# Two-piece split of keys, values and whole w_out blocks, and attention of the first unit ahead of later weight columns

## Chip, cores and metric

The kernel runs on one core of a Trainium2 chip. The metric is the device time of one launch in microseconds (us); lower is better. The engines are PE (TensorE, matmuls; PEld is its weight loads), DVE (VectorE), ACT (ScalarE), POOL (GpSimd) and SP (SyncE, which here only issues DMAs). Each engine works through its own list of instructions in a fixed order.

## The reference, cut to what is computed

```python
# attention: batch 4, heads 8, sequence 576, head size 64
scores = q @ k.T / 8
bias   = relu(x @ w1 + b1) @ w2      # x: a fixed function of the two positions; one bias per head
attn   = softmax(scores + bias)
x      = (attn @ v), heads side by side     # 2304 tokens x 512
# first feed-forward, hidden 1536
h = silu(x @ w_gate) * (x @ w_val);  x = h @ w_out
# second feed-forward, hidden 2048
h = relu(x @ w_in);  out = (h * h) @ w2_out
```

The large inputs of the feed-forwards are 64-bit numbers; keys, values and queries are 32-bit. Precision is kept by splitting each matrix into a 16-bit high part and a 16-bit low part ("hi" and "lo") and multiplying three of the four pairs.

## The kernel before, in words

**Units.** The 2304 tokens are worked in nine units of 256. A unit is one quarter of the sequence for two of the four batches (unit 8 holds the 64 last positions of all batches). `attend` makes the attention of a round: round 0 is the first sequence quarter for all four batches, and gives units 0 and 1. It has 32 steps, one per batch and head. In a step PE multiplies queries with keys (`scores`, L772), DVE adds the bias and finds the minimum (L780), ACT takes the exponential (L785) and its 16-bit part (L792), POOL the rest (L220, tile `pt`), an SP transpose turns both (L801, tile `pT`), and PE multiplies with the values (L812, two steps later). After 16 steps a unit is complete: `finish_unit` scales it and transposes it into `xT` (L857, L860).

**Keys and values.** For round 0 they come in eight groups of four heads (`h` 0 to 7). `load_kv` loads a group as 128 partitions x (4 heads x 4 rows x 64) and a tail of 64 partitions x (4 heads x 64). `prep_k` and `prep_v` split them with `halves`, in five chunks of 4 x 64 columns (`kv_chunks`). `halves` has three ways: way 1 makes hi on POOL (L197) and lo on DVE (L191); way 0 makes hi on ACT (L201) and lo on DVE (L191); way 2 scales on ACT (L205), makes hi on ACT (L209) and lo on POOL (L220). `MIX` says which: values always take way 1, key chunks take 0 and 2 in turn. Key chunks are then transposed by PE (`turn`, L686). Round 0 reads keys and values from these tiles (`wr`, `kva`, `kvb`); copies go to `kT_d` and `v_d` in HBM for the later rounds. `feed_first` calls the preparation of group h+1 at steps 4h (keys) and 4h+2 (values).

**Weights.** `w_stream` loads w_gate and w_val in three column blocks of 512 (`first`), then w_out in 12 row blocks of 128 x 512 (`second`, key "o"). Each block is decoded from 64-bit to 32-bit by three DVE operations (`decode`, L256, L259, L261), its columns' norms are taken, and it is split by `halves`. w_out blocks are decoded in two pieces of 256 columns, from four staging rooms in `wst`; from its eighth block on w_out waits for the last group's values ("kv", 8).

**moe1(m)** makes the first feed-forward of unit m: L453 for gate and val (needs `xT` of the unit and the weights' column block), L476 for w_out (needs all of w_out). `make_bias(t)` makes the bias of a round: masks on DVE (L597), matmuls on PE (L635), L611 and L617 on ACT, L612 and L618 on POOL. weights2 and the second feed-forward follow when all attention is done.

**What sets the order.** These parts are generators that yield a cost after each piece. `merge` takes the one whose sum of costs, divided by its weight, is least; `a_all` merges attention at weight 25.5 with the weights at 70. The lines of the loop at L1234 then mix that with moe1. The result is the program order; a list scheduler turns it into one list per engine with this order as the priority.

## Time and profile before

| | us |
|---|---|
| median of 3 runs | 1310.92 (1310.74 to 1312.64) |
| the profiled execution, its own time | 1316.36 |
| span of the profiled execution | 1314.6 |
| busy in that span: PE, DVE, ACT, POOL | 1105.3, 882.9, 633.6, 772.4 |

A profile row that groups instructions has the line, engine, operation and tiles, then the count, busy time in us, mean ns of one, and the engine's idle time just before with what ended it. The duration of an instruction on DVE or POOL includes time in which it has begun and cannot proceed. The view by stretches gives for each stretch of the span the busy time of every engine, the granted PE clock (1.00 is 2.4 GHz) and the mean busy share of the 16 DMA engines.

### The profile page before, as it was taken

Reading aid. Unit: us, or ns where it says so; the run is one execution under the profiler, and the core shown is the slowest. Engines: PE = TensorE matmul, PEld = TensorE weight load, DVE = VectorE, ACT = ScalarE, POOL = GpSimd, SP = SyncE. Lnnn points to the kernel's source line nnn. Section 1 sums busy time; section 2 is a strip of 40 time slices with the busy share of each in tenths; the row PEclk is TensorE's granted clock in tenths of the full one; section 3 lists DMA queues with packets and bytes.
Section 4 is the critical chain, followed back from the end, with each engine's and each line's share of the span. In section 5 each row is a group of like instructions: output and inputs, shape, how many; then the busy total and the mean of one; then the engine's idle time right before and its main releaser. Section 6 shows DMA issues by size and latency. Waiting matters only on the chain.

```text
span 1314.6 us, 27829 instructions
## 1 busy us (share of the span) xinstructions
PE 1105.3 (84%) x10676; PEld 806.6 (61%) x10676; DVE 882.9 (67%) x2042; ACT 633.6 (48%) x1316; POOL 772.4 (59%) x844
## 2 busy tenths in 40 slices
PE   3345556869899999999899987789977999999998
PEld 2334435656777868687685765647435658485687
DVE  6988887898666555657474533887788392754835
ACT  5546666647565565556565442437512341413322
POOL 4867644696986586757766450323898280724623
PEclk9998557769999999999999899899988999999999
DMA  8749997832999899998989994573001010020000
GB/s 235 184 125 186 227 239 187 189 84 52 214 216 215 184 198 178 196 212 171 183 176 202 228 232 118 180 213 96 16 0 33 33 33 33 0 49 17 17 34 16
DMA packets 329089, 177.47 MB, mean 135 GB/s; under 512 B 285052, under 2 KB 295292, under 8 KB 328956
## 3 DMA queue, kind: packets, MB, share of 16 engines
q1 hardware_dynamic: 328956, 175.70, 59.1%
q8 instruction: 83, 1.36, 0.4%
q14 instruction: 50, 0.41, 0.1%
HBM read 92.21 MB, written 19.48 MB: 85 GB/s over the span
## 4 chain that ended last, share of the span: by engine, by line
PE 44%; DVE 19%; DMA 16%; POOL 9%; issue 6%; ACT 4%; SPq 1%; POOLq 0%; ACTq 0%; DVEq 0%
PE mm L1290 11%; PE mm L1322 10%; PE mm L453 9%; PE mm L476 6%; DMA pT<-pt 5%; DMA qT<-qs 3%; PE av L812 3%; POOL pt L220 2%; PE qk L772 2%; DVE mask L597 2%; PE ma L1322 2%; DMA w2s<-in_moe_w_out_dram 1%; DVE wr L261 1%; DVE wr L191 1%; DVE s L780 1%
## 5 line engine op out<-in xcount | busy, mean ns | idle before, releaser
L453 PE MATMUL mm<-xT,wr 128*128 128x256 f16 x2376 | 297.2, 283 | 16.7 <-DVE th L464 10.3
L453 PEld LDWEIGHTS <-wr 128*128 128x128 f16 x2592 | 256.1, 101 | 69.6 <-issue 28.3
L1102 POOL TENSOR_TENSOR x<-x 128x256 f32<-128x256 f32 (+1 forms) x160 | 157.6, 993 | 155.2 <-ACT x L1299 149.9
L220 POOL TENSOR_TENSOR pt<-s,pt 128x576 f16<-128x576 f32 x144 | 189.3, 1317 | 69.0 <-ACT pt L792 58.0
L1290 PE MATMUL mm<-wr,w2r 128*128 128x512 f16 (+1 forms) x960 | 191.7, 362 | 10.6 <-ACT x L1295 10.6
L220 POOL TENSOR_TENSOR z<-th,z 128x256 f16<-128x256 f32 x108 | 83.9, 777 | 136.5 <-ACT z L438 133.6
L1290 PEld LDWEIGHTS <-w2r 128*128 128x128 f16 x960 | 94.7, 99 | 105.5 <-issue 16.2
L780 DVE CUSTOM_DVE_ANT_0 s<-qk,bias 128x576 f32<-128x576 f32 x144 | 107.7, 750 | 68.3 <-PE qk L772 47.1
L785 ACT ACTIVATE s<-s,sc 128x576 f32<-128x576 f32 x144 | 110.3, 772 | 88.8 <-DVE sc L784 74.3
L476 PE MATMUL mm<-wr,z 128*128 128x512 f16 x576 | 135.8, 380 | 1.9 <-DVE th L464 1.3
L812 PEld LDWEIGHTS <-pT 128*128 128x128 f16 (+3 forms) x2400 | 97.4, 104 | 57.4 <-DMA pT<-pt 34.0
L1322 PEld LDWEIGHTS <-wr 128*128 128x128 f16 x1134 | 111.0, 98 | 17.6 <-DVE wr L1102 2.5
L612 POOL TENSOR_TENSOR btmp<-btmp,xs 128x256 f32<-128x256 f32 (+1 forms) x108 | 81.7, 758 | 43.2 <-ACT btmp L611 39.4
L597 DVE TENSOR_TENSOR mask<-tabT,bias 128x1024 f16<-128x1024 f16 (+1 forms) x108 | 95.7, 901 | 12.3 <-PE ma L635 9.5
L812 PE MATMUL av<-vp,pT 128*128 128x65 f16 (+7 forms) x1920 | 85.4, 194 | 20.0 <-DMA pT<-pt 18.3
L1295 ACT ACTIVATE x<-mm 128x512 f32<-128x512 f32 (+1 forms) x80 | 43.4, 553 | 121.1 <-DVE wr L1102 69.4
L476 PEld LDWEIGHTS <-z 128*128 128x128 f16 x648 | 59.8, 98 | 65.1 <-issue 2.1
L1107 DVE CAST wr<-x 128x768 f16<-128x768 f32 (+3 forms) x60 | 61.1, 1022 | 36.0 <-ACT x L1299 22.9
L618 POOL TENSOR_TENSOR bias<-bias,btmp 128x256 f32<-128x256 f32 (+1 forms) x108 | 81.0, 752 | 5.9
L1102 DVE TENSOR_TENSOR wr<-x,wr 128x768 f16<-128x768 f32 (+3 forms) x60 | 80.4, 1343 | 1.9
L635 PEld LDWEIGHTS <-mask 128*128 128x128 f16 x1440 | 61.8, 106 | 30.5 <-issue 11.3
L1341 ACT ACTIVATE ob<-ob,fac 128x256 f32<-128x256 f32 x36 | 18.1, 507 | 108.0 <-DVE ob L1340 107.9
(257 smaller groups left out, 2038.5 us busy)
## 6 DMA issues: line engine op xcount, KB each, us to landing
vp<-v_d SPq DMA_DIRECT2D x64, 325.0 KB, 3.6
kp<-kT_d SPq DMA_DIRECT2D x64, 288.0 KB, 3.5
w2s<-in_moe_w_in_dram SPq DMA_DIRECT2D x16, 512.0 KB, 4.7
w2s<-in_moe_w_out_dram SPq DMA_DIRECT2D x16, 512.0 KB, 4.5
wr<-in_moe_w_gate_dram SPq DMA_DIRECT2D x24, 256.0 KB, 5.5
wst<-in_moe_w_out_dram SPq DMA_DIRECT2D x24, 256.0 KB, 4.0
wr<-in_moe_w_val_dram SPq DMA_DIRECT2D x24, 256.0 KB, 4.9
y_d<-yh SPq DMA_DIRECT2D x18, 256.0 KB, 3.8
```

What stands on the lines that cost most here:

```text
L220: nc.gpsimd.tensor_tensor(out=out_, in0=x, in1=hi, op=ALU.subtract)
L453: nc.tensor.matmul(pg[:, 256 * gi:256 * gi + 256], wr.parts(key, f // 4, cc, wl, P * (f % 4), P), mov(xl, cc), start=k == 0, stop=k == 11)
L476: nc.tensor.matmul(po, zall[:, f, zl, P * t:P * t + P], wr.parts("o", 0, f, wl), start=k == 0, stop=k == 3 * NF1 - 1)
L597: nc.vector.tensor_tensor(out=m[:, :, ni * e:ni * e + ni], in0=block(kb, i0, ni), in1=th, op=ALU.is_gt)
L612: nc.gpsimd.tensor_tensor(out=tmp[r], in0=tmp[r], in1=xb, op=ALU.mult)
L618: nc.gpsimd.tensor_tensor(out=bias[r, :, cs], in0=bias[r, :, cs], in1=tmp[r], op=ALU.add)
L780: nc.vector.tensor_tensor_reduce(out=s.rearrange("p (a j) -> p a j", a=2), in0=pq[:, :, 0:288], in1=bias[:, n].rearrange("p (a j) -> p a j ...
L785: nc.scalar.activation(s, s, AF.Exp, bias=nm, scale=-1.0)
L812: nc.tensor.matmul(av[r, slot, 0:cn], pT[:n, 5 * l + c, r], vs[e][:n, c, c0:c0 + cn], start=m == 0, stop=m == 14)
L1102: (nc.gpsimd if how else nc.vector).tensor_tensor(out=out_, in0=a, in1=b, op=op)
L1290: nc.tensor.matmul(ph[:, :n], w2r.parts("w", g // 4, cc, wl, P * (g % 4), P), yt[:, 4 * yl + cc, :], start=m == 0, stop=m == 11)
L1322: nc.tensor.matmul(po, HS[f][:, o:o + P], st["C7"][f][wl][:, b:b + 256], start=f == 0 and k == 0, stop=f == 7 and k == 2)
```

## The change

It has three parts. First, keys and values are split in two pieces a group and not five: 128 x 16 x 64 and the tail 64 x 4 x 64. `vv` is laid out by chunk (16 of them, then the 4 tails), so that the copy to `v_d` takes two DMAs, of which the second writes runs of 130 16-bit numbers (260 bytes). With two pieces a group `MIX` gives every large key piece way 0 and every key tail way 2. Second, w_out is decoded in whole blocks of 512 columns, from two staging rooms. Third, `merge` divides each new cost by a weight at that moment: attention has 1, the weights have 1.2 until unit 0 is finished and 2.4 from then on (70/25.5 is 2.75).

```diff
     def kv_chunks(f):
-        main = f[:, 0:1024].rearrange("p (h r d) -> p r h d", h=4, r=4)
-        tail = f[0:64, 1024:1280].rearrange("p (h d) -> p h d", h=4)
-        return [(P, r, main[:, r]) for r in range(4)] + [(64, 4, tail)]
+
+        x = f.rearrange("p (c d) -> p c d", d=D)
+        return [(P, 4, x[:, 0:16]), (64, 1, x[0:64, 16:20])]
...
-        for n, r, x in kv_chunks(kf):
-            o = ks[:n, r % 4]
+        for n, m, x in kv_chunks(kf):
+            o = ks[:n, 0:4 * m]
             halves(o[:, :, 0, :], o[:, :, 1, :], x, SQK, mixed("K"))
-            turn(kT[:, :, P * r:P * r + n], o.rearrange("p h l d -> p h (l d)"), 4, n)
+            for i in range(m):
+                r = i if m > 1 else 4
+                turn(kT[:, :, P * r:P * r + n], o[:, i::m].rearrange("p h l d -> p h (l d)"), 4, n)
...
-        for n, r, x in kv_chunks(vf):
-            halves(vv[:n, :, r, 64:128], vv[:n, :, r, 0:64], x, sv[:n], mixed("V"))
...
+        for n, m, x in kv_chunks(vf):
+            o = vv[:n, 0:16] if m > 1 else vv[:n, 16:20]
+            halves(o[:, :, 64:128], o[:, :, 0:64], x, sv[:n], mixed("V"))
...
-        nc.sync.dma_start(v_d[b][:, 4 * g:4 * g + 4], vv)
+        nc.sync.dma_start(
+            v_d[b][:, 4 * g:4 * g + 4, 0:4, :], vv[:, 0:16].rearrange("p (h r) w -> p h r w", h=4))
+        nc.sync.dma_start(v_d[b][:, 4 * g:4 * g + 4, 4, :], vv[:, 16:20])
...
-            x = min(free, key=lambda y: y[1] / y[2])
+            x = min(free, key=lambda y: y[1])
...
-                x[1] += c
+                x[1] += c / (x[2]() if callable(x[2]) else x[2])
...
     sg_o = Stage(
-        256, [wst[:, 512 * i:512 * i + 512].bitcast(I64) for i in range(4)],
+        512, [wst[:, 1024 * i:1024 * i + 1024].bitcast(I64) for i in range(2)],
...
-        yield from second(wr, "o", NF1, wo, kappa, sg_o, 4, mm)
+        yield from second(wr, "o", NF1, wo, kappa, sg_o, 2, mm)
...
-        yield from merge((sa, 25.5), (w_stream(), 70.0))
+        yield from merge((sa, lambda: 1.0), (w_stream(), lambda: 1.2 if done[0] < 0 else 2.4))
```

Three places of the engines' lists. Lines from L719 on carry numbers higher by 4 to 6 after the change (L780 is L786, L784 is L790, L801 is L807).

**DVE, values and keys of batch 1, second group** (`kvb`, L191 with `keep` is values, L191 without it is keys). Before:

```order
L670 TENSOR_SCALAR keep_1583<-ma 128x1
L674 TENSOR_SCALAR keep_1282<-keep_1583 128x1
L191 SCALAR_TENSOR_TENSOR kvb<-wr,keep_1583,kvb 128x4x64 x2
L191 SCALAR_TENSOR_TENSOR kvb<-wr,kvb 64x4x64
L191 SCALAR_TENSOR_TENSOR kvb<-wr,keep_1583,kvb 128x4x64 x2
L256 TENSOR_SCALAR wr<-wr 128x512
L191 SCALAR_TENSOR_TENSOR kvb<-wr,keep_1583,kvb 64x4x64
L191 SCALAR_TENSOR_TENSOR kvb<-wr,kvb 128x4x64
```

After:

```order
L670 TENSOR_SCALAR keep_1398<-ma 128x1
L786 ISA s,sc<-qk,bias 128x576
L786 ISA sc 128x1
L674 TENSOR_SCALAR keep_1138<-keep_1398 128x1
L712 TENSOR_SCALAR kvb<-kvb,keep_1398 128x20x2
L790 TENSOR_SCALAR sc<-sc 128x1
L832 TENSOR_SCALAR sc<-av,keep_1138 128x4
L835 RECIPROCAL sc<-sc 128x4
L256 TENSOR_SCALAR wr<-wr 128x512
L836 TENSOR_TENSOR kvb<-av,sc 128x256
L259 SCALAR_TENSOR_TENSOR wr<-wr 128x512
L191 SCALAR_TENSOR_TENSOR kvb<-wr,keep_1398,kvb 128x16x64
```

The scale of the values (L670) is followed at once by the first piece before; after the change a score, two decode rows and seven short ones stand between it and the one large piece, behind which the tail follows.

**DVE, around the 17th score row** (first step of batch 2; L780 is the score operation with its second, short row). Before:

```order
L780 ISA s,sc<-qk,bias 128x576
L780 ISA sc 128x1
L261 SCALAR_TENSOR_TENSOR wr<-wr 128x512
L150 TENSOR_SCALAR sc<-sc 1x1
L780 ISA s,sc<-qk,bias 128x576
L780 ISA sc 128x1
L741 COPY qs<-qs 128x4x64
L826 TENSOR_SCALAR sc<-av,keep_1282 128x4
L784 TENSOR_SCALAR sc<-sc 128x1
L256 TENSOR_SCALAR wr<-wst 128x256
```

After:

```order
L786 ISA s,sc<-qk,bias 128x576
L786 ISA sc 128x1
L790 TENSOR_SCALAR sc<-sc 128x1
L786 ISA s,sc<-qk,bias 128x576
L786 ISA sc 128x1
L667 TENSOR_TENSOR sc<-sc 128x1
L790 TENSOR_SCALAR sc<-sc 128x1
L786 ISA s,sc<-qk,bias 128x576
L786 ISA sc 128x1
L790 TENSOR_SCALAR sc<-sc 128x1
```

The decodes between the scores have gone to later places: from the first score row to the 17th there are 35 decode rows before and 20 after, and from the 17th to the 33rd 79 and 60 (w_out's own decode rows are 72 before and 36 after).

**SP, the copy of one group's values to HBM** (batch 1, first group; pT are the transposes of the attention weights). Before:

```order
L801 DMA_TRANSPOSE pT<-pt_118 128x10x128
L697 DMA kT_d_64<-kvb 128x2304
L712 DMA v_d_68<-kva 128x2600
L801 DMA_TRANSPOSE pT<-pt_119 128x10x128
L801 DMA_TRANSPOSE pT<-pt_117 128x10x128
```

After:

```order
L733 DMA qf<-in_q_dram 128x4x64
L277 DMA wr<-in_moe_w_val_dram 64x512
L714 DMA v_d_68<-kva 128x4x520
L716 DMA v_d_68<-kva 128x4x130
L807 DMA_TRANSPOSE pT<-pt_117 128x10x128
L807 DMA_TRANSPOSE pT<-pt_118 128x10x128
```

One DMA has become two, and the short-run one stands ahead of the transposes that follow.

## Rows read from the trace of the kernel before

**Rows 1.** View by stretches: stretch, length, busy (instructions) by engine, PEclk, DMA share, GB/s

```profile
core 0: us, PE busy (x) PEld busy (x) DVE busy (x) ACT busy (x) POOL busy (x), PEclk, DMA share, GB/s
0.00:91.20 91.20, 34.53 (x433) 28.79 (x433) 72.96 (x169) 49.01 (x114) 62.44 (x80) 1.00 0.69 179
91.20:166.10 74.90, 42.27 (x389) 30.07 (x390) 62.24 (x160) 45.24 (x85) 47.28 (x41) 0.69 0.95 210
166.10:222.10 56.00, 30.93 (x276) 22.57 (x275) 45.77 (x138) 34.64 (x74) 22.70 (x26) 0.59 0.92 231
222.10:265.00 42.90, 33.99 (x359) 27.36 (x357) 37.37 (x114) 30.72 (x63) 28.60 (x32) 0.84 0.74 160
265.00:320.90 55.90, 45.32 (x496) 31.93 (x496) 49.83 (x100) 30.68 (x69) 43.59 (x47) 0.82 0.22 56
320.90:790.00 469.10, 439.35 (x5331) 339.03 (x5328) 276.69 (x837) 263.01 (x552) 322.33 (x385) 0.99 0.97 199
```

**Rows 2.** Score operation on DVE by its line: ns min/median/max, first and last start

```profile
L780 DVE CUSTOM_DVE_ANT_0 s<-qk,bias x144: 721/750/760, 91.2 to 784.4; 128x576 f32<-128x576 f32 x144
```

**Rows 3.** Chain of waits, 318 to 322 us: start, us, what

```profile
320.95 0.76 DVE s L780
```

**Rows 4.** Groups by form, 0 to 321 us: key and value pieces

```profile
L220 POOL TENSOR_TENSOR kvb<-wr,kvb 128x256 f16<-128x256 f32 x16 | 20.0, 1252 | 14.8 <-ACT kvb L209 14.7
...
L191 DVE SCALAR_TENSOR_TENSOR kva<-wr,keep,kva 128x256 f16<-128x256 f32 x12 | 13.9, 1163 | 0.0
...
L191 DVE SCALAR_TENSOR_TENSOR kvb<-wr,keep,kvb 128x256 f16<-128x256 f32 x12 | 11.5, 992 | 1.0 <-POOL kvb L197 1.0
...
L197 POOL TENSOR_SCALAR kva<-wr,keep 128x256 f16<-128x256 f32 x12 | 10.2, 864 | 3.0 <-DVE keep L670 3.0
...
L197 POOL TENSOR_SCALAR kvb<-wr,keep 128x256 f16<-128x256 f32 x12 | 8.8, 749 | 0.7 <-DVE keep L670 0.7
...
L191 DVE SCALAR_TENSOR_TENSOR kvb<-wr,kvb 128x256 f16<-128x256 f32 x16 | 8.0, 500 | 3.9 <-ACT kvb L201 3.9
L191 DVE SCALAR_TENSOR_TENSOR wr<-wr,keep 128x256 f16<-128x256 f32 x8 | 7.5, 961 | 0.5 <-POOL wr L197 0.5
...
L197 POOL TENSOR_SCALAR wr<-wr,keep 128x256 f16<-128x256 f32 x8 | 4.8, 614 | 4.2 <-DVE keep L670 4.2
```

**Rows 5.** L191 by its line: ns min/median/max, first and last start, forms

```profile
L191 DVE SCALAR_TENSOR_TENSOR kvb<-wr,kvb x20: 407/409/886, 5.6 to 210.6; 128x256 f16<-128x256 f32 x16, 64x256 f16<-64x256 f32 x4
L191 DVE SCALAR_TENSOR_TENSOR kva<-wr,keep,kva x15: 465/474/3844, 117.1 to 232.8; 128x256 f16<-128x256 f32 x12, 64x256 f16<-64x256 f32 x3
```

**Rows 6.** Groups by form, 0 to 321 us: nearest larger pieces on ACT and POOL

```profile
L197 POOL TENSOR_SCALAR wr<-wr,keep 128x512 f16<-128x512 f32 x18 | 15.5, 860 | 10.9 <-DVE sc L784 4.1 <-DVE keep L291 3.5 <-DVE wr L191 3.1
...
L663 ACT ACTIVATE junk<-wr 128x1024 bf16<-128x1024 f32 x8 | 8.4, 1056 | 12.0 <-DMA wr<-in_v_dram 12.0
```

**Rows 7.** Groups by form, 0 to 321 us: decode operations, whole and w_out's halves

```profile
L261 DVE SCALAR_TENSOR_TENSOR wr<-wr 128x512 int32<-128x512 int32 x24 | 19.9, 832 | 0.0
L259 DVE SCALAR_TENSOR_TENSOR wr<-wr 128x512 int32<-128x512 int32 x24 | 19.4, 813 | 0.1
L256 DVE TENSOR_SCALAR wr<-wr 128x512 int32<-128x512 int32 x24 | 17.6, 736 | 5.9 <-DMA wr<-in_moe_w_val_dram 3.1 <-DMA wr<-in_moe_w_gate_dram 1.7 <-PE av L812 1.1
...
L261 DVE SCALAR_TENSOR_TENSOR wr<-wst,wr 128x256 int32<-128x256 int32 x24 | 15.0, 641 | 0.1
...
L259 DVE SCALAR_TENSOR_TENSOR wr<-wst,wr 128x256 int32<-128x256 int32 x24 | 10.3, 449 | 0.0
...
L256 DVE TENSOR_SCALAR wr<-wst 128x256 int32<-128x256 int32 x24 | 8.2, 361 | 5.0 <-PE mm L322 3.4 <-DMA wst<-in_moe_w_out_dram 1.2 <-POOL kvb L220 0.4
```

**Rows 8.** Timeline, 120 to 125 us: start, us, engine, line, operation

```profile
120.56 4.24 DVE L191 SCALAR_TENSOR_TENSOR kva<-wr,keep,kva 128x256 f16<-128x256 f32 x2
...
121.62 2.50 POOL L220 TENSOR_TENSOR pt<-s,pt 128x576 f16<-128x576 f32 x2
```

**Rows 9.** DMA issues by line: size each, median us from issue to landing

```profile
qf<-in_q_dram SPq DMA_DIRECT2D x32, 128.0 KB, 3.3
...
v_d<-kva SPq DMA_DIRECT2D x3, 650.0 KB, 3.3
```

More of the change, by code (lines that the diff above doesn't have):

```diff
@@ L705, in prep_v @@
         sv = st["sv", h]
-        for n, r, x in kv_chunks(vf):
-            halves(vv[:n, :, r, 64:128], vv[:n, :, r, 0:64], x, sv[:n], mixed("V"))
-        nc.gpsimd.memset(vv[:, :, :, 128:130], 1.0)
+        for n, m, x in kv_chunks(vf):
+            o = vv[:n, 0:16] if m > 1 else vv[:n, 16:20]
+            halves(o[:, :, 64:128], o[:, :, 0:64], x, sv[:n], mixed("V"))
+        nc.gpsimd.memset(vv[:, :, 128:130], 1.0)
         nc.vector.tensor_scalar(
-            out=vv[:, :, :, 128:130], in0=vv[:, :, :, 128:130], scalar1=sv, scalar2=None,
-            op0=ALU.mult)
-        nc.sync.dma_start(v_d[b][:, 4 * g:4 * g + 4], vv)
-        for i in range(2):
-            hold["v", b, 2 * g + i] = vv[:, 2 * i:2 * i + 2]
+            out=vv[:, :, 128:130], in0=vv[:, :, 128:130], scalar1=sv, scalar2=None, op0=ALU.mult)
+        nc.sync.dma_start(
+            v_d[b][:, 4 * g:4 * g + 4, 0:4, :], vv[:, 0:16].rearrange("p (h r) w -> p h r w", h=4))
+        nc.sync.dma_start(v_d[b][:, 4 * g:4 * g + 4, 4, :], vv[:, 16:20])
+        for i in range(4):
+            hold["v", b, 4 * g + i] = [vv[:, 4 * i + c] for c in range(4)] + [vv[:, 16 + i]]
         kv_used[0] = h + 1
@@ L755, in load_pair @@
         nc.sync.dma_start(vp, v_d[b][:, 2 * a:2 * a + 2])
-        hold["k", b, a], hold["v", b, a] = kp, vp
+        hold["k", b, a] = kp
+        for i in range(2):
+            hold["v", b, 2 * a + i] = [vp[:, i, c] for c in range(5)]
     def scores(t, b, n, kts):
@@ L812, in weighted @@
                     nc.tensor.matmul(
-                        av[r, slot, 0:cn], pT[:n, 5 * l + c, r], vs[e][:n, c, c0:c0 + cn],
+                        av[r, slot, 0:cn], pT[:n, 5 * l + c, r], vs[e][c][:n, c0:c0 + cn],
                         start=m == 0, stop=m == 14)
@@ L882, in avstep @@
                 hold["av"] = ps_av.tile([P, 4, P], F32, tag="av", name="av")
-            if merged:
-                vv = hold["v", b, n]
-                vs = [vv[:, e] for e in range(2)]
-            else:
-                vs = [hold["v", b, n // 2][:, n % 2]]
+            vs = [hold["v", b, 2 * n + e] for e in range(2)] if merged else [hold["v", b, n]]
             weighted(t, pT, hold["av"], s, vs)
@@ L999, in kvroom @@
         if h < 2:
-            kT, vv = [
-                wr.t.bitcast(F16)[:, 9 + 8 * h + o:13 + 8 * h + o, 0:n]
-                for o, n in ((0, S), (4, 5 * VW))]
-            vv = vv.rearrange("p h (c w) -> p h c w", c=5)
+            w = wr.t.bitcast(F16)
+            kT = w[:, 9 + 8 * h:13 + 8 * h, 0:S]
+            vv = w[:, 13 + 8 * h:17 + 8 * h, :].rearrange("p a b -> p (a b)")[:, 0:20 * VW].rearrange(
+                "p (c w) -> p c w", w=VW)
         else:
@@ L1006, in kvroom @@
             kT = r[:, 0:2304].rearrange("p (h s) -> p h s", h=4)
-            vv = r[:, 2304:4904].rearrange("p (h c w) -> p h c w", c=5, h=4)
-        ks = ba[:, 4904:4904 + 4 * 512].rearrange("p (r h l d) -> p r h l d", r=4, h=4, l=2)
+            vv = r[:, 2304:4904].rearrange("p (c w) -> p c w", w=VW)
+        ks = ba[:, 4904:4904 + 4 * 512].rearrange("p (c l d) -> p c l d", l=2, d=D)
         kf, vf = [wof[:, 3584 + 1280 * i:4864 + 1280 * i] for i in range(2)]
@@ L1020, in kv_start @@
         for h in range(4):
-            nc.gpsimd.memset(kvroom(h)[4][64:P, :, 4], 0.0)
+            nc.gpsimd.memset(kvroom(h)[4][64:P, 16:20], 0.0)
         for h in range(1):
```

## The prediction

> **What bounds the kernel now.** I read the view by stretches first, with its cuts at score rows of round 0: the first starts at 91.2 us [rows 2], the 33rd, which is the first of round 1, at 320.95 [rows 3]. In the five stretches up to there DVE is busy 72.96 + 62.24 + 45.77 + 37.37 + 49.83 = 268.2 of 320.9 us, 84% [rows 1]; PE is busy 187.0 us and runs at a granted clock of 0.59 to 0.84 from 91 us on, POOL 204.6, ACT 190.3. From 320.9 to 790 it is the other way round: PE 439.4 of 469.1 us (94%) at 0.99, DVE 59% [rows 1]. So up to 320.9 us DVE sets the pace, later PE does. All that the change removes or makes larger stands ahead of the 33rd score row in both lists: all eight groups of keys and values and all of w_out's decode. From that row on the lists of PE hold the same work in nearly the same places (it is matmul 1908 before and 1906 after). So what is gained by that row should come off the end, one for one, as long as PE, which takes over there, has no more left to do; and nothing that happens later can gain.
>
> **The change part by part.**
>
> *Keys and values on DVE.* As traced, the 48 pieces of 128x256 took 13.9 + 11.5 + 7.5 + 8.0 = 40.9 us [rows 4]; at the medians of L191, 409 ns for keys and 474 for values [rows 5], the same 48 take 16 x 0.409 + 32 x 0.474 = 21.7 us. The 19.2 us between are 0.40 us a piece in which it had begun and stood. No 1024-wide piece of this form is in the trace. A line through 256 columns in 409 ns [rows 5] and 576 in 750 [rows 2] has 1.07 ns a column, and gives an estimate of 1.23 us; 16 are 19.7 us. If every piece still stands 0.40 us, 16 cost 26.1 us: 14.8 us less. If the standing goes with the length instead, 19.7 x 40.9/21.7 = 37.1: 3.8 less. If nothing stood at either time, 2.0 less. I take 13, nearer to the first: in the piece that I can see stand, two of them took 4.24 us while POOL ran its `pt` row (2.50 us for two) beside them [rows 8], a wait for an instruction of the other engine and not for columns. Besides, four of the 12 tails (0.41 us each) go from DVE to POOL: 1.6 us.
>
> What the Trainium skill says of this ("SBUF — State Buffer", Who interferes with whom) is that a DVE instruction with two SBUF inputs and a GpSimd instruction that reads SBUF lock each other out for the whole instruction. Rows 8 agree. By it a wait is paid once an instruction, so fewer pieces pay fewer; but it speaks against large pieces as well, since one large POOL piece shuts DVE out for all its length.
>
> *w_out's decode.* 24 half-blocks took 15.0 + 10.3 + 8.2 = 33.5 us; 12 whole ones at 832 + 813 + 736 = 2381 ns, the means of the other weights' whole blocks, are 28.6: 4.9 us less [rows 7]. There are half as many loads of the same bytes, and two rooms hold as many bytes as four did, so no load starts later: nothing.
>
> *POOL.* The 32 value pieces took 10.2 + 8.8 + 4.8 = 23.8 us [rows 4]. Eight large ones cost no more than twice a 512-wide piece, 1.72 us each [rows 6]: 13.8, so 10 us less. The 16 key pieces of 20.0 us go altogether [rows 4]; four more tails come, at most 1.25 us each. POOL loses 25 us, but it was not the bound (64% busy). That relief can only make DVE stand less; I leave it out of the sum and keep it for the low end.
>
> *What is added to DVE's waits.* A large value piece on DVE waits for the whole hi piece on POOL, at most 1.72 us where the first small one waited for 0.6 to 0.9 [rows 4, 6]: 0.8 to 1.1 us more. In the list after, ten rows stand between the scale and that piece, a score (0.75 us) and two decode rows (0.74 and 0.81) among them [rows 2, 7], which cover it; where they do not, eight groups cost 8 us. Queued behind that piece on DVE are the next scores, for which ACT waits. I take 2 us. A large key piece is ready after 1.06 (ACT, [rows 6]) + 1.23 us. Its transposes are first read four steps later, and 32 steps took 230 us, so 29 us hide it: nothing; without that cover 7 groups x 1.5 us, 10 us.
>
> *The order.* Up to the 17th score row 15 decode rows fewer stand between DVE's scores, and unit 0 is ready earlier. That is work put off and not removed: between the scores of unit 1 stand the rows that were put off. For the 33rd row it is worth nothing by itself; before it, it lets moe1 of unit 0 start at a time when PE has room (30.9 of 56 us busy, [rows 1]).
>
> *The copy of the values.* SP issues eight DMAs more and 12 loads fewer. The tail DMA writes 512 runs of 260 bytes, 130 KB. The nearest row is the load of queries, 512 runs of 256 bytes, 128 KB: 3.3 us; the whole copy in one took 3.3 us too [rows 9]. Nobody reads `v_d` before round 1, so between 0 and 8 x 3.3 = 26 us I take 0; the far end is the second rival.
>
> *Sum.* DVE: -13 - 1.6 - 4.9 + 2 = -17.5 us; the ends are -2.0 - 1.6 - 4.9 + 8 = -0.5 and -14.8 - 1.6 - 4.9 = -21.3. DVE is busy 84% of the stage; the rest of the time it waits for loads and PE, and I let that share of the saving be lost: -15 us (-0.5 to -18). The profiled execution took 1316.4 us, 1.8 more than its span and 5.4 more than the median of the three runs; the same 15 us off the median, 1310.9, give **1296**.
>
> **The rivals.**
>
> *PE takes back most of it.* At w_out's first matmul in the list after, 104 matmuls of masks (L635) that stood ahead of it are still to come before the 33rd score row. At the mean of the last stretch, 45.32 us / 496 = 0.091 us [rows 1], they are 9.5 us. If PE, and not DVE, runs without a gap from there, 15 - 9.5 = 5 us are left: 1306. Against it speaks that the masks are made by DVE anyway and PE had 10 us idle in that stretch.
>
> *SP holds back attention.* SP's list is in order, and the new tail DMA stands ahead of `pT` transposes. If its 3.3 us come ahead of a waited-for transpose in every group, 26 us are added: 26 - 15 = 11 us slower, 1322. It decides from 15/8 = 1.9 us a group. For it: the DMA share is 0.92 to 0.95 from 91 to 222 us [rows 1]. Against: it has fallen to 0.22 in the last stretch, and the loads of the weights are spread over longer. The skill's "DMA: Bandwidth & Descriptors", Specifications, asks for 512 B or more in a transfer for line rate, which the tail's 260 B are not, so it stands on this rival's side; that queries of as short runs land in 3.3 us [rows 9] says that such a DMA is not slow by much.
>
> *POOL's relief counts in full.* Up to 320.9 us POOL loses 25 of 204.6 us, 12%. The four DVE groups of Rows 4 stood 19 us; decode means of 832 against 641 for double the width [rows 7] show that others stand too. If each us that POOL gives back lets DVE go on for half a us, 12 us more come off: 27 in all, 1284. For it: [rows 8]. Against: both engines wait for other things more often than for each other, and DVE stood long only where POOL had several rows in a queue.
>
> *The stage is not DVE's.* If loads and the scores' round trip through ACT, POOL and the transposes set round 0, DVE only gets more idle time: 0 to 2 us off, 1310. For it: PE at a granted clock of 0.59 to 0.69, its lower of two levels (1.2 and 2.4 GHz) for most of the time, makes that trip longer. Against: 84% busy, with POOL at 64%.
>
> **How the numbers follow.** The forecast (8 to 22 us off) has 0.52, POOL's relief in full 0.13, PE taking most back 0.10, the stage not DVE's 0.09, SP 0.16. About 0.2%, 2.6 us, is what a measurement of this kernel can tell from no change. Faster: 0.52 + 0.13 + 0.09 of PE's case = 0.74; within 0.2%: 0.09 and 0.01 of PE's = 0.10; slower 0.16. The range leaves out the slow case and the outermost of the relief: 1281 to 1313.
>
> **What would show it.** DVE's key and value pieces: 16 large ones of 1.2 to 1.7 us, 20 to 27 us in all; w_out's decode near 29 us. The first score row earlier by some us, the 33rd at 300 to 309 us, and from there to the end the same 994 us as before. The first moe1 matmul earlier by more than that. If the 33rd row comes 15 us earlier and the end does not, it is PE's later list, and my one-for-one is wrong. If large pieces take 2 us or more, the standing goes with length. If waits for `pT` on PE grow by some 20 us, it is SP. A 33rd row at its old place with DVE idle would be the last rival.

## The result, and the profile after

The changed kernel takes 1324.86 us (median of 4, 1321.35 to 1326.34) against 1310.83 for the kernel before (1309.54 to 1312.64): ratio 1.0088, 95% interval 1.0066 to 1.0111. By the ratio it is slower by 9 to 15 us; the prediction, 1296 with a range of 1281 to 1313, has the wrong sign. The profiled execution took 1326.34 us, with a span of 1324.6 (before 1314.6).

The view by stretches of the changed kernel, cut at its first, 17th, 25th, 29th and 33rd score row and at 790 us. The columns are those of [rows 1], and so are the cuts but for one: the 265.0 of [rows 1] is no score row, though the prediction calls its cuts so; the 29th row began at 246.5 us there.

```profile
core 0: us, PE busy (x) PEld busy (x) DVE busy (x) ACT busy (x) POOL busy (x), PEclk, DMA share, GB/s
0.00:77.50 77.50, 32.95 (x411) 27.17 (x412) 60.74 (x136) 40.23 (x83) 42.36 (x63) 1.00 0.73 185
77.50:142.50 65.00, 39.18 (x371) 28.01 (x371) 52.97 (x129) 43.10 (x76) 37.86 (x31) 0.81 0.95 215
142.50:204.90 62.40, 34.59 (x324) 25.91 (x323) 47.94 (x130) 36.66 (x70) 23.53 (x24) 0.63 1.00 232
204.90:255.80 50.90, 35.36 (x294) 26.55 (x293) 37.06 (x93) 26.51 (x56) 24.56 (x23) 0.73 0.57 138
255.80:322.00 66.20, 50.17 (x558) 34.77 (x557) 59.38 (x113) 37.08 (x79) 50.96 (x49) 0.82 0.38 83
322.00:790.00 468.00, 438.08 (x5268) 338.50 (x5267) 273.18 (x839) 265.59 (x554) 319.27 (x383) 0.98 0.96 195
```

The first score row comes 13.7 us earlier than in [rows 1], the 17th 23.6, the 25th 17.2. Then the gain is gone: the 29th is 9.3 us *later* (255.8 against 246.5) and the 33rd 1.1 later (322.0 against 320.95 in [rows 3]). DVE's busy time up to the 33rd row did fall, from 268.2 to 258.1 us, but its idle time rose from 52.7 to 63.9. From the 33rd row to the end of the span it is 1002.6 us, where the prediction wanted the same 994: of the 10 us between the two spans, 9 come after that row.

The pieces that the change makes, in the view of groups by form, 0 to 322 us (columns as in [rows 4] and [rows 7]):

```profile
L191 DVE SCALAR_TENSOR_TENSOR kvb<-wr,kvb 128x1024 f16<-128x1024 f32 x8 | 10.7, 1337 | 8.5 <-ACT kvb L201 8.5
L259 DVE SCALAR_TENSOR_TENSOR wr<-wst,wr 128x512 int32<-128x512 int32 x12 | 10.0, 841 | 0.0
L191 DVE SCALAR_TENSOR_TENSOR kvb<-wr,keep,kvb 128x1024 f16<-128x1024 f32 x3 | 8.6, 2869 | 0.0
L261 DVE SCALAR_TENSOR_TENSOR wr<-wst,wr 128x512 int32<-128x512 int32 x12 | 8.6, 722 | 0.0
L191 DVE SCALAR_TENSOR_TENSOR wr<-wr,keep 128x1024 f16<-128x1024 f32 x2 | 8.4, 4220 | 1.0 <-POOL wr L197 1.0
L256 DVE TENSOR_SCALAR wr<-wst 128x512 int32<-128x512 int32 x12 | 6.6, 562 | 9.5 <-DMA wst<-in_moe_w_out_dram 9.5
L191 DVE SCALAR_TENSOR_TENSOR kva<-wr,keep,kva 128x1024 f16<-128x1024 f32 x3 | 5.6, 1857 | 0.0
```

The 16 large pieces cost 10.7 + 8.6 + 8.4 + 5.6 = 33.3 us (40.9 before), w_out's decode 10.0 + 8.6 + 6.6 = 25.2 (33.5 before). The row of L256 shows a new wait: 9.5 us for w_out's loads.

What stands between the 28th and the 29th score row on PE, groups by line. First before (233.4 to 246.5 us), then after (213.6 to 255.8 us):

```profile
L453 PE MATMUL mm<-xT,wr 128*128 128x256 f16 x24 | 4.1, 349 | 0.0
```

```profile
L453 PE MATMUL mm<-xT,wr 128*128 128x256 f16 x129 | 21.7, 343 | 1.6 <-DVE th L464 1.6
...
L169 PE MATMUL mm<-sc,ones_r 1*128 1x2 f32 x4 | 1.2, 358 | 9.1 <-DVE sc L166 9.1
```

One step of moe1 (24 matmuls of L453) stood there; now there are more than five. In all, 4 steps of the first unit's moe1 stand ahead of the 29th score row before, 7 after.

The longest waits of the changed kernel from 195 to 322 us, first DVE's, then PE's (engine, line, waited for: us in total, times, longest):

```profile
DVE wr L256 <- DMA wst<-in_moe_w_out_dram: 9.5, 4, 3.1
DVE th L462 <- ACT th L461: 4.6, 3, 1.7
...
PE av L818 <- DMA pT<-pt: 10.5, 4, 5.1
PE mm L169 <- DVE sc L166: 9.1, 2, 5.4
```

These lines offer three suspects: the loads of w_out (two rooms), the order of the lists, and the transposes `pT` behind new DMAs on SP.

### The profile page after: what moved, and what is told of

The parts are those of the page before. It is cut to its first block, busy times and chain, and to the rows that moved or that the text cites. A ratio compares the mean times of both kernels' runs of the same rounds, so it can differ in the third digit from the quotient of the medians.

```text
span 1324.6 us, 27666 instructions
## 1 busy us (share of the span) xinstructions
PE 1117.0 (84%) x10676; PEld 810.9 (61%) x10676; DVE 871.3 (66%) x1970; ACT 629.9 (48%) x1280; POOL 747.0 (56%) x808
## 4 chain that ended last, share of the span: by engine, by line
PE 47%; DVE 19%; DMA 16%; POOL 7%; issue 6%; ACT 3%; SPq 2%; POOLq 0%; ACTq 0%; DVEq 0%
PE mm L453 11%; PE mm L1292 11%; PE mm L1324 9%; PE mm L476 5%; DMA pT<-pt 4%; PE av L818 3%; DMA qT<-qs 2%; PE qk L778 2%; POOL pt L220 2%; DVE mask L597 2%; DMA w2s<-in_moe_w_in_dram 2%; PE ma L1324 2%; DMA wst<-in_moe_w_out_dram 2%; DMA wr<-in_v_dram 1%; DVE wr L259 1%
## 5 line engine op out<-in xcount | busy, mean ns | idle before, releaser
L453 PE MATMUL mm<-xT,wr 128*128 128x256 f16 x2400 | 303.0, 284 | 10.1 <-DVE th L464 6.5
L453 PEld LDWEIGHTS <-wr 128*128 128x128 f16 x2592 | 259.2, 103 | 64.9 <-issue 19.9
L1104 POOL TENSOR_TENSOR x<-x 128x256 f32<-128x256 f32 (+1 forms) x160 | 157.7, 994 | 155.1 <-ACT x L1301 149.9
L220 POOL TENSOR_TENSOR pt<-s,pt 128x576 f16<-128x576 f32 x144 | 193.3, 1348 | 72.1 <-ACT pt L798 60.5
L786 DVE CUSTOM_DVE_ANT_0 s<-qk,bias 128x576 f32<-128x576 f32 x144 | 107.9, 751 | 72.6 <-PE qk L778 52.1
```

The source lines that it names most:

```text
L220: nc.gpsimd.tensor_tensor(out=out_, in0=x, in1=hi, op=ALU.subtract)
L453: nc.tensor.matmul(pg[:, 256 * gi:256 * gi + 256], wr.parts(key, f // 4, cc, wl, P * (f % 4), P), mov(xl, cc), start=k == 0, stop=k == 11)
L786: nc.vector.tensor_tensor_reduce(out=s.rearrange("p (a j) -> p a j", a=2), in0=pq[:, :, 0:288], in1=bias[:, n].rearrange("p (a j) -> p a j ...
L1104: (nc.gpsimd if how else nc.vector).tensor_tensor(out=out_, in0=a, in1=b, op=op)
```

## The experiments

**The theories.** A: two rooms for whole w_out blocks make each decode wait for its load. B: the new order puts the decode of the late weights in one heap ahead of the 29th score row. C: the large pieces and the two copies of values hold back SP or POOL. D, formed after the first runs: the order costs by a side effect. moe1 is mixed with the rest by a table of leads (`LEAD`), counted from a point that the program takes when the first unit is done:

```python
if done[0] >= 0 and w_done[0] >= 0 and base is None:
    base = pos["a"]
lead = base is not None and pos["a"] >= base + float(np.interp(pos["m"], *LEAD))
```

`pos["a"]` adds up the costs of attention *and* of the weights. The new rule has fewer weights done when the first unit is, so `base` is 88.2 and not 92.4 (sums of the planner's costs, no times). The table is unchanged, so for the rest of the program moe1 stands 4.2 further ahead of attention: by the table 0.7 of a step for the first unit and 1.4 to 1.9 steps later (a step of moe1 has the cost 2.6).

All ratios are to the kernel before on the same chip, with the 95% interval in brackets; a table behind the runs has the marks of the traces. What the expectations call the 28th score row (246.5 us before, 255.8 after) is the 29th of this text; their 33rd is the same.

**1. The parts alone and in pairs.** `b_kv` is the kernel before with the change's lines on keys and values alone:

```diff
+        return [(P, 4, x[:, 0:16]), (64, 1, x[0:64, 16:20])]
```

> The kernel before with only the split of keys and values in two pieces a group (and the two copies of the values to DRAM that go with it); w_out's half-blocks with four rooms and the old order of the two streams stay. Theory A (the two rooms of whole w_out blocks make each decode wait for its load): this part costs nothing, DVE's 48 pieces of 40.9 us become 16 of about 33, the 33rd score row comes 5 to 10 us before 320.9, and the time is 1301 to 1306 us against 1310.8. Theory B (the new order puts the decode of the weights in one heap ahead of the 28th score row): the same, 1301 to 1306. Theory C (the large pieces and the two copies hold back SP or POOL): slower, 1313 to 1325.

Measured 1.0000 (0.9982 to 1.0018), which none of the three theories had; the 33rd row came 3 us later, not earlier. `b_wo` has w_out's rooms alone:

```diff
-        256, [wst[:, 512 * i:512 * i + 512].bitcast(I64) for i in range(4)],
+        512, [wst[:, 1024 * i:1024 * i + 1024].bitcast(I64) for i in range(2)],
```

> The kernel before with only w_out in whole blocks, two staging rooms and two loads ahead. Theory A: a load of 512 KB starts only when a whole block is decoded and lands 4 to 7 us later; in the old order the decodes of w_out stand further apart, so it waits less than in the changed kernel but more than before: DVE's wait for w_out's loads grows from 1.2 us to 5 to 10, the saved decode (33.5 to 25 us) is lost, and the time is 1309 to 1316. Theory B: the rooms are without effect, and the 8 us of decode that are saved show: 1302 to 1306. Theory C: the same as B.

Measured 1.0039 (1.0017 to 1.0061), some 1316 us: the upper end of A, and not B or C. DVE's wait for the loads grew to 3.3 us (195 to 322 us), less than A said. `b_ord` has the order alone:

```diff
-        yield from merge((sa, 25.5), (w_stream(), 70.0))
+        yield from merge((sa, lambda: 1.0), (w_stream(), lambda: 1.2 if done[0] < 0 else 2.4))
```

> The kernel before with only the new rule by which attention of the first unit and the stream of weights are put in one order. Theory A: with four rooms no decode waits long for its load; scores up to the 24th come 10 to 15 us earlier, the 33rd stays within 5 us of 320.9, and the time is 1306 to 1313. Theory B: the 28th score row is already late here (255 us against 246.5), and the time is 1318 to 1325. Theory C: as A.

Measured 1.0186 (1.0160 to 1.0212): slower, which B alone had said, and by about twice as much as B gave. `kv_ord` is the changed kernel without the new rooms:

```diff
-        512, [wst[:, 1024 * i:1024 * i + 1024].bitcast(I64) for i in range(2)],
+        256, [wst[:, 512 * i:512 * i + 512].bitcast(I64) for i in range(4)],
```

> The changed kernel with only w_out put back to half-blocks, four rooms and four loads ahead. Theory A: the wait of DVE for w_out's loads (9.5 us in four waits) goes, the 28th score row comes at 235 to 245 us instead of 255.8, the 33rd at 305 to 315 instead of 322.0, and the time is 1300 to 1312 instead of 1324.9. Theory B: nothing of that goes; 1318 to 1326. Theory C: 1318 to 1326, with v_d's copies ahead of waited-for transposes.

Measured 1.0085 (1.0060 to 1.0110), the same as the whole change and as B and C said. DVE's wait for w_out's loads fell to 1.6 us, and PE waited in another place instead (its profiled execution, 1317.4 us, lies 6 us under its other five):

```profile
DVE wr L256 <- DMA wst<-in_moe_w_out_dram: 1.6, 2, 1.3
...
PE mm L169 <- DVE sc L166: 11.1, 2, 10.6
PE av L818 <- DVE kvb L836: 7.1, 1, 7.1
```

So theory A falls: without the rooms the loss is the same, and the longest new wait in the profile after is not its cause. `kv_wo` is the changed kernel with the old order:

```diff
-        yield from merge((sa, lambda: 1.0), (w_stream(), lambda: 1.2 if done[0] < 0 else 2.4))
+        yield from merge((sa, 25.5), (w_stream(), 70.0))
```

> The changed kernel with the old order of attention and weights (and so with base at 92.4): split of keys and values and w_out in whole blocks stay. Alone the split gave a ratio of 1.000 and the whole blocks 1.0039. Theories B and D both put the loss down to the order: ratio 0.990 to 1.005, 1300 to 1320 us. Theory A: the two rooms cost as much here as in the changed kernel, ratio 1.006 or more.

Measured 0.9965 (0.9940 to 0.9990), as B and D said. The loss is the order's.

**2. The point from which moe1's lead counts.** `lead_early` is the kernel before with one edit:

```diff
-            base = pos["a"]
+            base = pos["a"] - 4.2
```

> The kernel before, where the point from which moe1's lead over attention is counted (base, 92.4 in its own units when the first unit is done) is set 4.2 lower, to the 88.2 that it has in the changed kernel; nothing else. Theory D (the new order of attention and weights costs its time because it lowers this point, which puts moe1 one to two steps of 24 matmuls further ahead of attention in the lists for the rest of the run): slower than before by 0.6% to 2%, 1320 to 1337 us, with the 13th moe1 step of DVE over 10 us later than 329. Theory B (it is the decode of the late columns and of w_out that stands in one heap between the 27th and the 28th score row): within 0.3% of before, 1309 to 1317.

Measured 1.0127 (1.0094 to 1.0160), as D said; moe1's 13th step came at 336.9 us, 8 later and not over 10. `ord_lead` and `after_lead` are `b_ord` and the changed kernel with the opposite:

```diff
-            base = pos["a"]
+            base = pos["a"] + 4.2
```

> The kernel before with the new order of attention and weights alone, and base raised by 4.2, so that moe1's lead is counted from 92.4 as before. With the order alone the ratio was 1.0186. Theory D: most of it goes, ratio 0.998 to 1.008, 1311 to 1324 us. Theory B: it stays, ratio 1.014 to 1.02, 1331 to 1339.

> The changed kernel whole, with base raised by 4.2 to the 92.4 that it had before; nothing else. Theory D: the loss of the order goes and the gain of the large pieces is left, ratio to before 0.988 to 0.998, 1297 to 1311 us. Theory B: as the changed kernel, ratio 1.006 to 1.011, 1321 to 1328. Theory A (rooms of w_out): the same as B.

Measured 1.0063 (1.0041 to 1.0085) where `b_ord` had 1.0186, and 0.9947 (0.9924 to 0.9970) where the change had 1.0088. Both fit D. B left these kernels where they were, so it is not the main cause; it may own what is left, since in `ord_lead` the 29th row still comes at 260.3 us. The waits for w_out's loads in `after_lead`, with the same two rooms, and those for `pT`, 195 to 322 us:

```profile
DVE wr L256 <- DMA wst<-in_moe_w_out_dram: 2.8, 2, 1.7
...
PE av L818 <- DMA pT<-pt: 8.1, 3, 5.4
```

The 9.5 us for loads were a consequence of where moe1 stood, too: with only the first unit's steps moved (`after_u0`, below) they are 2.7 us, with only the others moved (`after_rest`) 8.2.

**3. How much lead, and the rooms and the copy again.** `lead_late` is the kernel before with `base` + 4.2, `after_lead8` the changed kernel with `base` + 8.4:

```diff
-            base = pos["a"]
+            base = pos["a"] + 8.4
```

> The kernel before with base raised by 4.2 (to 96.6); nothing else. Lowering it by 4.2 cost 1.27%. Theory D as a plain slope (the later moe1 is counted from, the better): 0.5% to 1.3% faster, 1296 to 1307 us. Theory D with a best place at the old point (the table of leads was made for it): 0 to 1% slower, 1313 to 1326.

> The changed kernel with base raised by 8.4 (to 96.6) instead of 4.2. At 88.2 the ratio to before was 1.0088, at 92.4 it was 0.9947. As a plain slope: 0.980 to 0.990, 1287 to 1300 us. With a best place near 92.4: 0.993 to 1.005, 1304 to 1320.

Measured 1.0050 (1.0028 to 1.0073) and 1.0025 (1.0008 to 1.0043): later is worse as well, so it is a best place and no slope. In both orders 92.4 is the best of the three points tried. At 96.6 the time is lost behind attention: from the first load of the second weights to the end the two kernels take 514 and 515 us, all others 504 to 510. `kv_ord_lead` is `kv_ord` with `base` + 4.2:

> The changed kernel with base at 92.4 and w_out back in half-blocks with four rooms and four loads ahead. The same with whole blocks and two rooms had the ratio 0.9947. Theory A (two rooms of whole blocks cost waits for loads): faster than that by 3 to 10 us, ratio 0.987 to 0.992. If the saved decode outweighs the waits: slower than it by 2 to 8 us, ratio 0.996 to 1.001. If they cancel: 0.993 to 0.996.

Measured 0.9931 (0.9908 to 0.9954), which overlaps with `after_lead`: rooms and saved decode cancel. `vtail2x` is `after_lead` with the copy of the values' tail issued twice:

```diff
         nc.sync.dma_start(v_d[b][:, 4 * g:4 * g + 4, 4, :], vv[:, 16:20])
+        nc.sync.dma_start(v_d[b][:, 4 * g:4 * g + 4, 4, :], vv[:, 16:20])
```

> The changed kernel with base at 92.4, in which the second copy of the values (the 64-row tail, 130 KB) is issued twice for each of the eight groups, the second time with the same bytes. It prices the prediction's rival that this copy on SP's list holds back the transposes of attention: by that rival one copy costs up to 3.3 us a group, so eight more cost 10 to 26 us, ratio 1.002 to 1.015. If the copy is hidden: within 3 us of the same without it, ratio 0.992 to 0.997.

Measured 0.9919 (0.9895 to 0.9943), a little under what was expected of a hidden copy: eight more of these DMAs cost nothing that can be measured, so in this order the copy's own time is hidden. It does not price a copy that waits for its piece on DVE and so holds up what stands behind it in SP's list. The Trainium skill ("DMA: Bandwidth & Descriptors", Specifications) asks for 512 B or more for line rate; runs of 260 B did no harm here, where 130 KB is little.

**4. Where the earlier moe1 costs.** `after_u0` counts the lead of the changed kernel from 92.4 for the first unit's steps alone, `after_rest` for all others alone; `early_u0` and `early_rest` lower it in the kernel before for the same two stretches. The edit of `after_u0` is this; the others have `0.0 if pos["m"] < 46 else 4.2`, `-4.2 if pos["m"] < 46 else 0.0` and `0.0 if pos["m"] < 46 else -4.2` in its place:

```diff
-        lead = base is not None and pos["a"] >= base + float(np.interp(pos["m"], *LEAD))
+        lead = base is not None and pos["a"] >= base + (4.2 if pos["m"] < 46 else 0.0) + float(np.interp(pos["m"], *LEAD))
```

> The changed kernel with moe1's lead counted from 92.4 for the steps of the first unit alone, and from 88.2 for all later units. Lead from 88.2 throughout gave the ratio 1.0088, from 92.4 throughout 0.9947. If the loss lies where the first unit's moe1 stands among the decode of the late columns and w_out (up to the 33rd score row, 10 us of the 24 us between the two profiled executions): 0.9990 to 1.003. If it lies wholly there: 0.993 to 0.997. If wholly in the later units: 1.006 to 1.010.

> The mirror image: the changed kernel with the lead counted from 88.2 for the first unit and from 92.4 for all later units. If the loss is shared as the two profiled executions share it (10 us up to the 33rd row, 14 us after it): 0.999 to 1.004. If it lies wholly in the first unit: 1.006 to 1.010. If wholly in the later units: 0.993 to 0.997.

> The kernel before with the lead counted 4.2 earlier for the first unit's steps alone. Counted 4.2 earlier throughout the ratio was 1.0127. By the profiled executions 12 of 11 us lie up to the 33rd score row, so most of the loss should be here: 1.008 to 1.014. If it is shared: 1.004 to 1.008; if it is wholly in the later units: 0.998 to 1.002.

> The kernel before with the lead counted 4.2 earlier for all units but the first. If most of the loss is the first unit's: 0.998 to 1.003. If it is shared: 1.004 to 1.008; if it is wholly in the later units, where fewer of moe1's steps are left for the time in which the second weights are made: 1.010 to 1.014.

Measured 1.0030 (1.0006 to 1.0053), 1.0028 (1.0007 to 1.0048), 1.0073 (1.0049 to 1.0096) and 1.0054 (1.0034 to 1.0075). All four lie where they were expected if the loss is shared between the two halves, and these add up in both kernels: 0.58% + 0.60% = 1.18% beside the 1.41% from 1.0088 to 0.9947, and 0.73% + 0.54% = 1.27% beside 1.27%. There are two places, of 7 to 10 us each.

The first place is the stage up to the 33rd row: it comes at 332.0 us in `early_u0` and 318.6 in `early_rest` (before 320.9), at 314.0 in `after_u0` and 323.4 in `after_rest` (change 322.0, `after_lead` 312.0). It is not in every pair: with the new order and half-blocks the two points differ by 2 to 3 us there (`kv_ord` 316.3 and `kv_ord_lead` 314.4, `b_ord` 329.4 and `ord_lead` 326.5). How this place loses its time is not shown. The count of moe1 steps ahead of the 29th row does not tell it: 7 in the change, 8 in `after_lead`.

The second is the end of attention. SP's timeline, the first loads of the second weights (start, us, what), in the changed kernel and in `after_lead`:

```profile
820.16 11.47 SPq L277 DMA_DIRECT2D w2s<-in_moe_w_in_dram  x6
```

```profile
795.97 9.19 SPq L277 DMA_DIRECT2D w2s<-in_moe_w_in_dram  x5
```

DVE's wait for them from 780 to 945 us, in the same two:

```profile
DVE w2r L256 <- DMA w2s<-in_moe_w_in_dram: 17.0, 6, 10.9
```

```profile
DVE w2r L256 <- DMA w2s<-in_moe_w_in_dram: 5.3, 4, 2.5
```

The 50 us from the last score row on, in the same two:

```profile
790.70:840.70 50.00, 35.02 (x321) 22.81 (x320) 20.67 (x63) 12.76 (x28) 3.96 (x5) 0.83 0.54 145
```

```profile
772.60:822.60 50.00, 39.94 (x350) 26.83 (x345) 24.17 (x75) 13.62 (x30) 4.96 (x6) 0.90 0.50 144
```

The last `av` matmuls of attention, in the chain of waits of the same two (770 to 830 and 750 to 805 us):

```profile
801.35 0.80 PE av L818 x30
```

```profile
779.25 1.48 PE av L818 x60
```

From the last score row to that load it is 29.5 us (790.7 to 820.2) against 23.4 (772.6 to 796.0). Of the 6 us, 3 lie ahead of the end of the last `av` (802.15 and 780.73) and 3 behind it. One step more of moe1 stands ahead of the last score row (84 against 83). DVE then waits 10.9 us in one piece, PE is busy 35 of 50 us and not 40, and its granted clock there is 0.83 instead of 0.90. All six kernels that count the later units from the lower point have 84 steps there and 27.2 to 29.5 us from the last score row to the load, all twelve that count them from 92.4 have 83 steps and 23.4 to 24.1 us. The 73rd to the 97th step of moe1 take 156 to 163 us in the six and 148 to 154 us in the twelve. Why the one step more delays the loads by 3 to 6 us, and where the rest of this half lies, is open.

**5. Is DVE the pace?** `less_dve` is the kernel before and `less_dve_lead` is `after_lead`, in which two of w_out's three decode operations are left out:

```diff
+        if short:
+            return
         nc.vector.scalar_tensor_tensor(
             out=t, in0=hi, scalar=-0x40000000, in1=t, op0=ALU.bitwise_and, op1=ALU.bitwise_or)
```

> The kernel before, where two of the three decode operations of w_out's half-blocks (lines 259 and 261, 48 operations, 25.3 us of DVE's busy time up to the 33rd score row) are left out, so that w_out's decoded values are wrong; the rest is done as ever. It tests the step that DVE sets the pace of the first stage and passes on 84% of what it is spared. If that holds: the 33rd score row at 296 to 304 us instead of 320.9, ratio 0.981 to 0.987, 1288 to 1296 us. If the stage is held by the whole round of PE, ACT, POOL, DVE and loads in their fixed lists: the row at 310 to 321, ratio 0.992 to 1.000.

> The changed kernel with base at 92.4 (ratio 0.9947, 33rd score row at 312.0), where the same two of three decode operations of w_out's whole blocks are left out, 24 operations and some 19 us of DVE's time; w_out's decoded values are wrong, the rest is done as ever. If DVE passes on 84%: 16 us less, the row at 296, ratio 0.980 to 0.985. If the stage is not DVE's: the row at 304 to 312, ratio 0.989 to 0.996.

Measured 1.0066 (1.0040 to 1.0092), *slower* than the kernel with all of the work and outside both expectations, and 0.9902 (0.9874 to 0.9931), 6 us less than `after_lead` for some 20 us of DVE's time, as expected if the stage is not DVE's (its 33rd row comes at 303.2 us, 8.8 earlier). The stretch up to the 33rd row, first in the kernel before, then in `less_dve`:

```profile
0.00:320.90 320.90, 187.04 (x1948) 140.72 (x1949) 268.16 (x675) 190.29 (x402) 204.62 (x225) 0.80 0.71 171
```

```profile
0.00:331.90 331.90, 191.86 (x2025) 146.92 (x2026) 253.70 (x636) 193.07 (x409) 194.72 (x227) 0.81 0.69 167
```

25.3 us of operations are gone, DVE is busy 14.5 us less, and the row comes 11 us later. The scheduler has sorted the lists anew: 7 steps of moe1 instead of 4 now stand ahead of the 29th score row, which comes at 261.6 us. That this sorting is the cause is argued from the trace; no run holds the lists fixed, and none sorts them anew with all else equal. So how far a mere change of places moves the time is not known; `less_dve` and `b_wo`, which spare DVE work and lose 0.66% and 0.39%, suggest that it can be half of what `base` does. Against that as the whole of D stand three kernels that moved as D said, and the halves that add up in two.

**The traces side by side.** One profiled execution each, us from the span's start; "base" is where the lead counts from (two numbers: first unit, later units), "steps" the count of moe1 steps whose DVE row (L464) stands ahead of the 29th score row, "ahead" the same for the 144th and last, "to load" the time from that row to the first load of the second weights, "73 to 97" the time between those steps of moe1. The times of one kernel spread by 6 us and more from execution to execution, so a single difference of a few us shows nothing.

| kernel | ratio | base | steps | 28th score | 29th | 33rd | 144th | ahead | to load | 73 to 97 |
|---|---|---|---|---|---|---|---|---|---|---|
| before | 1 | 92.4 | 4 | 233.4 | 246.5 | 320.9 | 784.4 | 83 | 23.5 | 152.3 |
| b_kv | 1.0000 | 92.4 | 7 | 223.1 | 254.5 | 324.0 | 782.8 | 83 | 23.5 | 148.4 |
| b_wo | 1.0039 | 92.4 | 5 | 230.8 | 255.5 | 327.5 | 785.0 | 83 | 23.6 | 149.9 |
| b_ord | 1.0186 | 88.2 | 7 | 233.4 | 264.3 | 329.4 | 798.8 | 84 | 27.5 | 157.6 |
| kv_ord | 1.0085 | 88.2 | 7 | 216.2 | 251.4 | 316.3 | 782.4 | 84 | 27.2 | 156.5 |
| after | 1.0088 | 88.2 | 7 | 213.6 | 255.8 | 322.0 | 790.7 | 84 | 29.5 | 162.8 |
| kv_wo | 0.9965 | 92.4 | 8 | 223.0 | 255.8 | 322.2 | 775.8 | 83 | 23.4 | 148.0 |
| lead_early | 1.0127 | 88.2 | 10 | 235.2 | 267.9 | 333.2 | 789.6 | 84 | 27.3 | 158.3 |
| ord_lead | 1.0063 | 92.4 | 8 | 230.3 | 260.3 | 326.5 | 783.2 | 83 | 23.5 | 147.7 |
| after_lead | 0.9947 | 92.4 | 8 | 212.0 | 245.9 | 312.0 | 772.6 | 83 | 23.4 | 149.5 |
| lead_late | 1.0050 | 96.6 | 4 | 226.2 | 249.0 | 324.7 | 783.2 | 79 | 23.9 | 155.2 |
| after_lead8 | 1.0025 | 96.6 | 4 | 213.7 | 237.8 | 314.0 | 776.9 | 80 | 22.2 | 145.3 |
| kv_ord_lead | 0.9931 | 92.4 | 5 | 212.2 | 240.0 | 314.4 | 775.4 | 83 | 23.5 | 149.8 |
| vtail2x | 0.9919 | 92.4 | 5 | 212.4 | 237.4 | 312.7 | 774.9 | 83 | 23.4 | 148.8 |
| after_u0 | 1.0030 | 92.4, 88.2 | 8 | 214.0 | 247.8 | 314.0 | 777.7 | 84 | 27.5 | 161.8 |
| after_rest | 1.0028 | 88.2, 92.4 | 7 | 217.0 | 258.5 | 323.4 | 782.8 | 83 | 23.4 | 150.1 |
| early_u0 | 1.0073 | 88.2, 92.4 | 10 | 234.1 | 265.7 | 332.0 | 794.3 | 83 | 24.1 | 150.0 |
| early_rest | 1.0054 | 92.4, 88.2 | 4 | 231.5 | 244.6 | 318.6 | 788.5 | 84 | 27.3 | 161.0 |
| less_dve | 1.0066 | 92.4 | 7 | 231.2 | 261.6 | 331.9 | 794.3 | 83 | 23.5 | 152.2 |
| less_dve_lead | 0.9902 | 92.4 | 5 | 210.6 | 233.4 | 303.2 | 766.4 | 83 | 23.4 | 153.5 |

`after_lead`, `kv_ord_lead` and `vtail2x` are faster than the kernel before by 0.5% to 0.8%, `kv_wo` by 0.35%.

## Why the prediction was wrong, point by point

**"For the 33rd row it is worth nothing by itself", on the order: the step that failed.** The order alone costs 1.86%, and the term that the sum lacks is `base`: 1.2% to 1.4%, shown from both sides (`lead_early`; `ord_lead` and `after_lead`). The prediction looked at which decode rows stand between which scores and at the count of matmuls ahead of the 33rd row (1908 and 1906 by its count), and took equal counts for equal places. But moe1 had moved against attention: one step more stands ahead of the last score row wherever the later units count from the lower point. With `base` put back the change gains 0.5%, some 7 us, where 15 were forecast. What is left of the order with `base` mended is 0.6% in the kernel with small pieces (`ord_lead`) and 0.2% of gain in the changed one (`after_lead` against `kv_wo`, less than their intervals can tell apart).

**"Up to 320.9 us DVE sets the pace": failed.** A busy share of 84% was read as the bound, at a rate of 0.84 us for each us spared. `less_dve` shows the wrong sign and `less_dve_lead` a rate of 0.4 at the 33rd row and 0.3 at the end. That the stage is a round of PE, ACT, POOL, DVE and loads through lists that are fixed when the kernel is built, and that an edit sorts those lists anew, fits both but is argued. The rival "the stage is not DVE's" (0.09) described this, and its sign is in the profile: the 33rd row near its old place, with DVE idle for longer. It foresaw 0 to 2 us of gain, and no loss.

**Keys and values: half right.** The key pieces took 1.34 us in the mean against an estimate of 1.23. The eight large value pieces took 8.6 + 8.4 + 5.6 = 22.6 us, 2.8 each: they still stand behind POOL, as the one in [rows 8] did. So 7.6 us were saved and not 13. The price of a large piece was right: the nine that did not stand behind POOL took 1.20 to 1.27 us. The standing was not: 0.40 us a piece spread over all 48 what few of them paid. In the trace before, ten pieces of over 0.8 us hold 16.8 of the 19.2 us; in the trace after, seven of the 16 stand, and for 13.7 us. The count of waits fell from ten to seven, not to a third, and each is as long as what POOL does meanwhile. By the sign that the prediction gave (2 us or more, and it is 2.08 in the mean) the standing goes with length; it lies between its two cases (26.1 and 37.1 us). As a part the split is worth nothing in the old order (`b_kv`) and 1.0% to 1.3% in the new one (1.0186 to 1.0085; 1.0063 to 0.9931), 13 to 17 us. Why the old order returns nothing is not settled: `b_kv` has 7 steps ahead of the 29th row as `less_dve` has, but `kv_wo` gains with 8.

**w_out: size off, and one sentence wrong.** The decode lost 8.3 us, not 4.9. "No load starts later: nothing" was wrong as read from the trace (waits of 9.5 us for 1.2 before) and right in the sum of the changed kernel: with or without the rooms the time is the same, at either `base` (`kv_ord`, `kv_ord_lead`). In the old order it is not: the whole blocks cost 0.39% with small pieces (`b_wo`) and gain 0.35% with large ones (`kv_wo` against `b_kv`).

**"What is gained by that row should come off the end, one for one": failed in part.** The second place of the loss, at the end of attention, lies after that row. The prediction held that nothing later could change. The changed kernel has lost 1.1 us at the 33rd row and 10.0 at the end of the span; `after_lead` has gained 8.9 and 14.2.

**The rivals.** SP (0.16) had the right time, 1322, but not the reason: the copy's own time costs nothing in `vtail2x`, and the loss goes with `base` while the copy stays. PE's waits for `pT` up to the 33rd row grew from 8.5 to 18.5 us, half of the sign that the prediction gave for it; with the same copies they are 11.0 in `kv_ord`, which loses as much as the change, and 13.0 in `after_lead`, which gains. A chance on the right number would not have been a right reading. POOL lost the 25 us that were forecast (204.6 to 179.3 busy), and no gain of that size followed. PE's taking back is not seen: `after_lead` gains more at the end than at the 33rd row.

## What to carry to other kernels

When a change re-weights a merge, look for everything else that reads the same running sum: a start point, a table tuned for it, a due time. Compare lists by what stands ahead of the rows that others wait for, not by how many rows stand there. Where a scheduler sorts the lists, a busy share is no price for an engine's work; take a known piece of that work away and measure, and when a suspect wait shows up in the profile after, remove it alone before believing it.

## What was unexpected of the hardware

A DVE piece that meets a run of POOL rows can stand until the run is over, whatever its own length. Timeline of the changed kernel (start, us, engine, operation):

```profile
261.58 1.57 POOL L197 TENSOR_SCALAR kvb<-wr,keep 128x1024 f16<-128x1024 f32 x2
262.74 4.59 DVE L191 SCALAR_TENSOR_TENSOR kvb<-wr,keep,kvb 128x1024 f16<-128x1024 f32 x1
263.12 0.66 POOL L220 TENSOR_TENSOR z<-th,z 128x256 f16<-128x256 f32 x1
263.75 2.50 POOL L220 TENSOR_TENSOR pt<-s,pt 128x576 f16<-128x576 f32 x2
```

POOL's last row ends at 266.25 and the piece at 267.33, 1.08 us later. Four POOL rows had passed: one that ran when the piece began, and three that followed it. Another piece, which began at 51.75, ended 1.07 us behind a run of POOL rows that ended at 54.90. But DVE does not always wait for all that POOL has to do. Here it comes in between two rows, and POOL's second row stands instead, 1.65 us where the same row took 0.66 above:

```profile
231.10 1.56 POOL L220 TENSOR_TENSOR wr<-wr 128x512 f16<-128x512 f32 x1 [2.41 <-ACT wr L209]
231.57 2.97 DVE L191 SCALAR_TENSOR_TENSOR kva<-wr,keep,kva 128x1024 f16<-128x1024 f32 x2
232.62 1.65 POOL L220 TENSOR_TENSOR z<-th,z 128x256 f16<-128x256 f32 x1
```

What decides between the two is not shown. The Trainium skill ("SBUF — State Buffer", Who interferes with whom) says that a DVE instruction with two SBUF inputs contends with a GpSimd instruction that reads SBUF, and calls the ports that they share an exclusive lock. The trace agrees (the piece ends 1.07 to 1.09 us behind POOL's last row in all seven that stood), and adds that one wait can hold several rows. This is why the 16 large pieces saved less than one equal wait for each piece that was dropped.
